# Strassen's seven block products for the first product of the second expert layer, in three of its five token blocks

## The chip, the cores and the metric

One Trainium2 chip, one core of it. The metric is device time of one execution in microseconds (us), lower is better. The engines are named as the profile names them: PE is TensorE's matmul, PEld its weight load, DVE VectorE, ACT ScalarE, POOL GpSimd, SP the engine whose queue issues most transfers.

## What is computed

```
a = attention(q, k, v, M_prev, z_prev, beta)     # 4 x 8 heads, 576 tokens, 64 wide
x = a as 2304 tokens x 512
h = x @ w_in;   x = (h * cos(h)) @ w_out         # first expert layer: 512 -> 2048 -> 512
h = x @ w2_in;  r = max(h, 0)
out = (r * r) @ w2_out                           # second expert layer, the same shapes
```

All of it is in float32. A float32 product is made of three fp32r matmuls: each operand is split into a part that fp32r holds exactly (hi) and the rest (lo), and hi·hi, hi·lo and lo·hi are summed in PSUM.

## The kernel before

Attention runs first and takes until about 193 us; the two layers follow. The 2304 tokens lie in five blocks of 512, 512, 512, 256 and 512 (`CFG['sizes']`), the 2048 hidden features in 16 f-tiles of 128. A **step** (`steps`, line 280) is a layer, a block and an f-tile. Phase 1, the first layer, is steps 0 to 79; phase 2, the second layer, is steps 80 to 159, its blocks in the order 0, 1, 2, 4, 3 (`order2`, line 69), so the block of 256 tokens comes last.

In a step `l1` (line 293) makes the first product: for each of four slices of 128 input features three matmuls of 128 x n into `h`, n being the block's tokens; twelve in all. Then comes a chain on ACT and DVE (`g_a` to `g_g`, lines 318 to 369). In phase 2 this is `relu` on ACT, its square on DVE, the hi part `gh` on ACT, and `gl = gf - gh` on DVE. Two steps later (`skew`) `l2` (line 863) adds the f-tile's part of the second product into four PSUM banks `a0` to `a3`, which hold 128 tokens x 512 each in phase 2: twelve matmuls of 512 columns, or six for the block of 256 tokens. After a block's last f-tile `evac` (line 901) copies these to SBUF and stores them.

The order of the instructions on each engine is written out: for every step the templates in `CFG['tpl']` list tokens (L1, a, b, f, g, L2 and so on, each with a lag in steps), and `_Pinned` (line 34) keeps each engine in the order of the calls. So nearly every instruction has line 48. Weights of the second layer are converted from float64 words during phase 1, stored to DRAM and loaded again, split (`split_hi`, `split_lo`) in steps 64 to about 83, and then stay in SBUF: `winh`, `winl`, `wouth`, `woutl` for each f-tile. The activations between the layers go through DRAM (`x1T`); `x_load`, `x_hi` and `x_lo` (lines 240 to 273) bring a block's 512 features back as four `xh`/`xl` pairs.

Of the kernel before, what the change touches and what calls it, by code (L numbers as in the profile page):

```python
# [33 lines left out]
class _Pinned:  # L34
# [5 lines left out]
    def __getattr__(self, name):  # L40
# [83 lines left out]
def kernel(  # L124
# [15 lines left out]
    S = (qk.shape[3] - 128) // 2  # L140
    NT, DM = out.shape
# [117 lines left out]

    def x_hi(phase, j, kk, raw):  # L260
        n = blocks[j][1]
        hi = xs.tile([128, 512], F32R, tag=f"xh{kk}", name=f"xh{kk}")
        lo = xs.tile([128, 512], F32R, tag=f"xl{kk}", name=f"xl{kk}")
        act.activation(out=hi[:, span(n)], in_=raw[:, 0:n], func=AF.Copy)
        xt[phase, j, kk] = (hi, lo)
        return hi, lo, raw, n
# [4 lines left out]
            out=lo[:, span(n)], in0=raw[:, 0:n], in1=hi[:, span(n)].bitcast(F32), op=ALU.subtract  # L271
        )

    ps_s = ctx.enter_context(tc.tile_pool(name="ps_s", bufs=2, space=PSUM))
# [6 lines left out]
    opens = {(p, j, a) for p, j, a, e in segs}  # L281
    closes = {(p, j, e - 1) for p, j, a, e in segs}
    xneed, s0 = {}, 0
    for p, j, a, e in segs:
        if a == 0 and s0:
# [573 lines left out]
    def moe(ctx, g_o, early):  # L859
        ps_a = ctx.enter_context(tc.tile_pool(name="psa", bufs=1, space=PSUM))  # L860
        acc, part = {}, {}

        def l2(s):
            p, j, f = steps[s]
            n = blocks[j][1]
            hi, lo = wt[p, "out", f]
            gh, gl = gs.pop(s)
            na = KD if p == 1 else n // 128
            if (p, j, f) in opens:
                for c in range(na):  # L870
                    acc[c] = ps_a.tile([128, 512], F32, tag=f"a{c}", name=f"a{c}")
            for c in range(na):
# [13 lines left out]

        def evac_tile(c):
            if c < 2:
                return g_o.tile([128, 512], F32, tag="ob", name="ob")
            return wr.tile([128, 512], F32, tag="wl", name="ob", bufs=2)  # L890

        got = {}
# [8 lines left out]
        def evac(s):  # L901
# [4 lines left out]
            for c in range(KD if p == 1 else n // 128):  # L906
                cs = slice(c * 128, (c + 1) * 128)
                w = n if p == 1 else DM
                if s == len(steps) - 1 and c == n // 128 - 1:
                    for x, e in enumerate((sync, act)):  # L910
                        hc = slice(x * 256, (x + 1) * 256)
                        ob = evac_tile(2 + x)
                        copy("D", ob[:, hc], acc[c][:, hc])
                        e.dma_start(out=out[t0 + c * 128:t0 + (c + 1) * 128, hc], in_=ob[:, hc])
                    continue
                if (j, c) in got:
                    ob = got.pop((j, c))
                    dve.tensor_tensor(out=ob, in0=acc[c], in1=ob, op=ALU.add)
                else:
                    ob = evac_tile(c)  # L920
# [9 lines left out]
        for e in (pe, act, dve, pool, sync):  # L930
            e.last = None
        SK = CFG["skew"]
        N = len(steps)
# [5 lines left out]
        raws, convs, stores, backs, xs_at = [], {}, {}, {}, {}  # L939
# [24 lines left out]
        def step(name, u, s):  # L964
            live = u < N
            if name == "L1":
                if live and u >= early:
                    l1(u)
            elif name == "L2":
                if live:  # L970
                    l2(u)
                    l2_done.add(u)
            elif name in "abcdsefg":
                if live:
                    g_do(name, u)
            elif name == "k0":
                if raws and u in plan:
                    it, raw = raws.pop(0)
                    convs[u] = (it, *c_steps(raw), {})
            elif name[0] == "k":  # L980
                if u in convs:
                    it, wf, ops, made = convs[u]
                    x = int(name[1])
                    assert all(y in made for y in {2: (1,), 3: (2,), 4: (3,), 6: (4, 5)}.get(x, ()))
                    made[x] = True
                    ops[x - 1]()
                    if name == "k6" and s + 1 < free_at(it):
                        stores[u] = convs.pop(u)
            elif name in ("h0", "h1", "h2", "o0", "o1", "o2"):
                src = convs if name[1] == "0" else backs  # L990
                key = u if name[1] == "0" else (u, int(name[1]))
                if key in src:
                    it, wf, made = src[key][0], src[key][1], src[key][-1]
                    if name[0] == "h":
                        assert name[1] != "0" or 6 in made
                        made["h"] = split_hi(it[0], wf, it[1], it[2])
                    else:
                        split_lo(it[0], wf, made["h"], it[1], it[2], CFG["lo"][it[0] - 1])
            elif name == "ld":
                raw_next()  # L1000
            elif name in ("r1", "r2"):
# [102 lines left out]
```

## Time and profile before

| | before |
|---|---|
| time, median of 3 runs (lowest, highest) | 981.21 us (980.02, 981.24) |
| time of the profiled execution | 980.61 us |
| span of that execution (first to last instruction) | 978.9 us |
| PE busy | 971.3 us (99%), 5454 matmuls |
| DVE, ACT, POOL busy | 588.5 us (60%), 542.3 us (55%), 166.0 us (17%) |
| moved by DMA | 95.87 MB, mean 98 GB/s |

How to read it: "busy" of PE counts a matmul until its modelled end, so matmuls that follow each other overlap in it; the time that a matmul costs is the distance from its start to the next one's. In a row of the timeline the first number is the start, the second the duration. A bracket at the end gives the idle time before it and what ended it.

### The profile page before, as it was taken

The page shows a single profiled execution, that of the slowest core. Times are in us where ns is not written, and L with a number is a line of the kernel's source. Part 1 is how long each engine was busy: PE and PEld are TensorE (multiplying, and loading weights), DVE is VectorE, ACT ScalarE, POOL GpSimd, SP SyncE. Part 2 cuts the span into 40 slices and gives each one's busy share as a digit, 9 for nine tenths or more (in the row PEclk, how much of TensorE's full clock was granted, in tenths as well). Part 3 has the DMA queues.
Part 4 walks back from the last instruction along what each step waited for, and adds up shares of the span by engine and source line. Part 5 has one row for each costly group of instructions (what it writes and reads, how often), then busy time and mean ns, then how long its engine had stood idle before and what let it go on. Part 6 is the DMA issues. An engine that isn't in the chain of part 4 may idle for free.

```text
span 978.9 us, 14925 instructions
## 1 busy us (share of the span) xinstructions
PE 971.3 (99%) x5454; PEld 796.6 (81%) x5454; DVE 588.5 (60%) x1249; ACT 542.3 (55%) x1135; POOL 166.0 (17%) x247
## 2 busy tenths in 40 slices
PE   8999999999999999999999999999999999999998
PEld 5777777788888888889988888888888888888897
DVE  7988888588899667678887885323232323222232
ACT  7999998777777656666767773222222222222222
POOL 7777875300111000001000000000000000000000
PEclk9999999999999999999999999999999999999999
DMA  6345654453324433343355552001000100100010
GB/s 196 125 166 187 214 194 144 159 151 108 107 86 138 143 108 108 104 144 126 123 172 153 181 167 82 22 0 65 10 13 1 65 21 2 54 1 12 1 44 22
DMA packets 54699, 95.87 MB, mean 98 GB/s; under 512 B 5730, under 2 KB 26722, under 8 KB 54626
## 3 DMA queue, kind: packets, MB, share of 16 engines
q1 hardware_dynamic: 54192, 94.50, 29.8%
q8 instruction: 43, 0.70, 0.3%
q10 hardware_dynamic: 434, 0.43, 0.1%
q14 instruction: 30, 0.25, 0.1%
HBM read 70.00 MB, written 24.90 MB: 97 GB/s over the span
## 4 chain that ended last, share of the span: by engine, by line
PE 95%; DVE 3%; ACT 1%; issue 1%; DMA 0%; DVEq 0%; POOL 0%; POOLq 0%
PE h L48 39%; PE a L48 39%; PE o L48 6%; PE sps L48 5%; PE ptps L48 5%; PE qps L48 2%; DVE gf L48 1%; DVE wa L48 1%; DVE P L48 0%; DVE wb L48 0%; ACT gf L48 0%; DMA x1T<-ob 0%; ACT ki L48 0%; ACT P L48 0%; ACT gh L48 0%
## 5 line engine op out<-in xcount | busy, mean ns | idle before, releaser
L48 PE MATMUL h<-xh,winh 128*128 128x512 f32 (+1 forms) x640 | 236.0, 369 | 0.2 <-DVE gf L48 0.2
L48 PE MATMUL h<-xh,winl 128*128 128x512 f32 (+1 forms) x640 | 235.0, 367 | 0.0
L48 PE MATMUL h<-xl,winh 128*128 128x512 f32 (+1 forms) x640 | 235.0, 367 | 0.0
L48 DVE TENSOR_TENSOR gf<-gf 128x512 f32<-128x512 f32 (+1 forms) x80 | 51.1, 639 | 269.9 <-ACT gf L48 269.9
L48 ACT ACTIVATE gf<-h 128x512 f32<-128x512 f32 (+1 forms) x80 | 44.4, 556 | 287.2 <-PE h L48 287.2
L48 PEld LDWEIGHTS h<-xh,winh 128*128 128x128 f32 x640 | 120.2, 188 | 21.5 <-DVE gf L48 0.6
L48 PEld LDWEIGHTS h<-xl,winh 128*128 128x128 f32 x640 | 120.1, 188 | 20.4
L48 PEld LDWEIGHTS h<-xh,winl 128*128 128x128 f32 x640 | 120.5, 188 | 19.9
L48 PE MATMUL a<-gl,wouth 128*128 128x512 f32 (+1 forms) x320 | 117.8, 368 | 0.1
L48 PE MATMUL a<-gh,wouth 128*128 128x512 f32 (+1 forms) x319 | 117.1, 367 | 0.3 <-DVE ob L48 0.3
L48 PE MATMUL a<-gh,woutl 128*128 128x512 f32 (+1 forms) x320 | 117.4, 367 | 0.0
L48 PE MATMUL a<-woutl,gh 128*128 128x512 f32 x288 | 112.0, 389 | 0.0
L48 PE MATMUL a<-wouth,gl 128*128 128x512 f32 x288 | 112.0, 389 | 0.0
L48 PE MATMUL a<-wouth,gh 128*128 128x512 f32 x288 | 112.0, 389 | 0.0
L48 ACT ACTIVATE gh<-gf 128x512 fp32r<-128x512 f32 (+1 forms) x160 | 93.4, 584 | 33.1 <-DVE gf L48 32.1
L48 DVE TENSOR_TENSOR gl<-gf,gh 128x512 fp32r<-128x512 f32 (+1 forms) x158 | 102.0, 645 | 4.2 <-ACT gh L48 2.5
L48 POOL TENSOR_SCALAR wa<-wa 128x512 f32<-128x512 f32 x63 | 40.0, 634 | 364.8 <-ACT wa L48 334.8
L48 POOL TENSOR_SCALAR P<-P,sm 128x384 f32<-128x384 f32 (+3 forms) x128 | 87.0, 697 | 29.2 <-ACT x L48 20.1
L48 ACT ACTIVATE ki<-h 128x512 int32<-128x512 f32 (+1 forms) x80 | 44.2, 552 | 64.7 <-PE h L48 64.3
L48 DVE TENSOR_TENSOR gf<-h,gf 128x512 f32<-128x512 f32 (+1 forms) x80 | 50.7, 634 | 47.6 <-ACT ki L48 41.0
L48 ACT ACTIVATE P<-P,mx 128x384 f32<-128x384 f32 (+3 forms) x128 | 70.5, 560 | 2.5 <-DVE mx L45 2.5
L48 PEld LDWEIGHTS a<-gl,wouth 128*128 128x128 f32 x320 | 60.1, 188 | 10.8 <-DVE gl L48 0.6
(95 smaller groups left out, 1478.9 us busy)
## 6 DMA issues: line engine op xcount, KB each, us to landing
wraw<-in_moe_w_in_dram SPq DMA_DIRECT2D x32, 512.0 KB, 4.1
wraw<-in_moe_w_out_dram SPq DMA_DIRECT2D x32, 512.0 KB, 3.8
qk<-in_qk_dram SPq DMA_DIRECT2D x15, 640.0 KB, 5.3
vr<-in_vrow_dram SPq DMA_DIRECT2D x16, 320.0 KB, 5.6
xT<-x SPq DMA_DIRECT2D x16, 288.0 KB, 2.3
out_dram<-ob SPq DMA_DIRECT2D x17, 256.0 KB, 2.2
x1T<-ob SPq DMA_DIRECT2D x16, 256.0 KB, 2.3
xraw<-x1T SPq DMA_DIRECT2D x16, 256.0 KB, 3.1
```

The lines of the kernel that those rows point to most:

```text
L48: made = call(*args, **kwargs)
```

## The change

In phase 2 the blocks come in the order 0, 3, then 1, 2, 4. Blocks 0 and 3 are steps 80 to 111 (`NS` is 112) and run as before. For blocks 1, 2 and 4 (512 tokens each) the first product is made for two f-tiles at a time: the 256 hidden features x 512 input features by 512 input features x 512 tokens are cut into 2 x 2 blocks of 256, and seven products of these blocks (Winograd's variant) give the result in place of eight. There are 8 pairs per block, 24 in all, numbered k.

Beside that: the sums of weight blocks (s1 to s4) are made on POOL during steps 85 to 100 from the stored weights, split by ACT and DVE into hi and lo, and stored to DRAM (`s_load` to `s_store`). For this every second-layer w_in tile is now stored. In the pairs of the first block s1 is loaded over the weight half that is no longer needed (`s_place`), and for every pair 768 KB of s2, s3 and s4 come back through two sets of buffers (`r_load`). The sums of activation blocks (t1 to t4) are made on POOL (`t_make`), for the first block in steps 105 to 108, for the other two during the block before, and split on ACT and DVE (`x_h`, `x_l`). All x tiles live in one SBUF tile `xb`. The four PSUM banks that held `h` become `h0` to `h3` of 256 columns each; `combine` adds up products that PSUM can't add itself, and `g_sq` does relu and square in one DVE instruction.

```diff
-       'order2': [0, 1, 2, 4, 3],
+       'order2': [0, 3],
+       'seven': [1, 2, 4],
...
+    xb = xs.tile([128, 14 * 512 + 64], F32R, name="xb", bufs=1)
...
+        def s_sum(q):
+            wa, wb = sums[q]
+            t = [g_p.tile([128, 512], F32, tag="ki", name="sf") for _ in range(2)]
+            a11, a12, a21, a22 = wa[:, 0:256], wa[:, 256:512], wb[:, 0:256], wb[:, 256:512]
...
+            for o, x, y, op in (
+                (s1, a21, a22, ALU.add), (s2, s1, a11, ALU.subtract),
+                (s3, a11, a21, ALU.subtract), (s4, a12, s2, ALU.subtract),
+            ):
+                pool.tensor_tensor(out=o, in0=x, in1=y, op=op)
...
+        def s_split(q):
...
+            for x, h, _ in hl:
+                act.activation(out=h, in_=x, func=AF.Copy)
+            for x, h, l in hl:
+                dve.tensor_tensor(out=l, in0=x, in1=h.bitcast(F32), op=ALU.subtract)
...
+        def s_place(q):
+            hi, lo = wt[2, "in", 2 * q]
+            sync.dma_start(out=hi[:, 0:256].bitcast(F32), in_=spilled["s", q, 2][:, 0:256])
+            sync.dma_start(out=lo[:, 0:256].bitcast(F32), in_=spilled["s", q, 2][:, 256:512])
...
+        def r_load(k):
+            q = k % (NF // 2)
+            r1 = wr.tile([128, 2 * DM], F32R, tag="wraw", name="r1")
+            r2 = wr.tile([128, DM], F32R, tag="wa", name="r2", bufs=2)
+            sync.dma_start(out=r1.bitcast(F32), in_=spilled["s", q, 0])
+            sync.dma_start(out=r2.bitcast(F32), in_=spilled["s", q, 1])
...
+        def product(k, i):
+            w, x, bank, first = {
+                1: ("a11", "b11", k % 2, True), 2: ("a12", "b21", 2, True), 7: ("s3", "t3", 3, True),
+                6: ("s2", "t2", k % 2, False), 4: ("a22", "t4", 3, False), 5: ("s1", "t1", k % 2, False),
+                3: ("s4", "b22", k % 2, False),
+            }[i]
...
+            for kt in range(2):
+                ws, xc = slice(128 * kt, 128 * kt + 128), slice(256 * kt, 256 * kt + 256)
+                for n, (lt, rt) in enumerate(((wh, xh), (wh, xl), (wl, xh))):
+                    pe.matmul(
+                        out=banks[bank], lhsT=lt[:, ws], rhs=rt[:, xc],
...
+        def combine(k, x):
+            a, c, d = banks[k % 2], banks[2], banks[3]
+            if x == "c11":
+                ha[k] = g_p.tile([128, 512], F32, tag="gf", name="ha")
+                act.activation(out=ha[k][:, 0:256], in_=c, func=AF.Copy)
+                dve.tensor_tensor(out=ha[k][:, 0:256], in0=a, in1=ha[k][:, 0:256], op=ALU.add)
+            elif x == "p7":
+                p7[k] = wr.tile([128, DM], F32, tag="wc", name="p7", bufs=1)
+                act.activation(out=p7[k][:, 0:256], in_=d, func=AF.Copy)
+            elif x == "u2":
+                act.activation(out=p7[k][:, 256:512], in_=a, func=AF.Copy)
+            elif x == "c21":
+                hb[k] = g_p.tile([128, 512], F32, tag="ki", name="hb")
+                dve.tensor_tensor(out=hb[k][:, 0:256], in0=d, in1=p7[k][:, 256:512], op=ALU.add)
+            elif x == "c22":
+                dve.tensor_tensor(out=hb[k][:, 256:512], in0=a, in1=p7[k][:, 0:256], op=ALU.add)
+            else:
+                act.activation(out=ha[k][:, 256:512], in_=a, func=AF.Copy)
...
+            dve.scalar_tensor_tensor(out=h, in0=h, scalar=0.0, in1=h, op0=ALU.max, op1=ALU.mult)
...
+        for k in range(K):
+            s0 = NS + 2 * k
...
+            if k + 1 < KP:
+                s_place(k + 1)
+            if 0 < k and k + 1 < K:
+                r_load(k + 1)
...
+            if k > 0:
+                combine(k - 1, "c12")
+            product(k, 1)
+            if k > 0:
+                g_sq(k - 1, 1)
+            product(k, 2)
+            combine(k, "c11")
...
+            product(k, 7)
+            combine(k, "p7")
...
+            l2(s0 - 2)
...
+            product(k, 6)
+            combine(k, "u2")
+            product(k, 4)
+            combine(k, "c21")
...
+            l2(s0 - 1, (0, .5))
+            evac(s0 - 1, (0, .5))
+            product(k, 5)
+            combine(k, "c22")
...
+            g_sq(k, 0)
...
+            if k < K - 1:
+                l2(s0 - 1, (.5, 1))
+                evac(s0 - 1, (.5, 1))
+            product(k, 3)
+            if k == K - 1:
+                l2(s0 - 1, (.5, 1))
...
+            g_do("f", s0)
+            g_do("g", s0)
```

Three places show how the instructions move. The first is PE's order for a first product in block 1. Before, one f-tile's product has twelve such rows; these are the first six (two of the four slices of input features).

```order
L48 MATMUL h<-xh_5992,winh_5966 128x512
L48 MATMUL h<-xl_5993,winh_5966 128x512
L48 MATMUL h<-xh_5992,winl_5988 128x512
L48 MATMUL h<-xh_6109,winh_5966 128x512
L48 MATMUL h<-xl_6110,winh_5966 128x512
L48 MATMUL h<-xh_6109,winl_5988 128x512
```

Now, products 2 and 7 of a pair (bank `h2`, then bank `h3`; `r1` and `r2` are the loaded sums of weights):

```order
L48 MATMUL h2_7660<-xb_79,winh7_6052 128x256 x2
L48 MATMUL h2_7660<-xb_79,winl7_6070 128x256
L48 MATMUL h2_7660<-xb_79,winh7_6052 128x256 x2
L48 MATMUL h2_7660<-xb_79,winl7_6070 128x256
L48 MATMUL h3_7661<-xb_79,r1_7846 128x256 x2
L48 MATMUL h3_7661<-xb_79,r2_7847 128x256
L48 MATMUL h3_7661<-xb_79,r1_7846 128x256 x2
L48 MATMUL h3_7661<-xb_79,r2_7847 128x256
```

A product is six matmuls of 256 columns, so a pair has 42 of these in place of 24 of 512 columns, with the second product's matmuls of 512 columns between them.

The second place is the hand-over inside a pair, on PE and DVE. On PE: product 5 into bank `h0`, half of a second product, and product 3 into the same bank, which waits for DVE.

```order
L48 MATMUL h0_7658<-xb_79,winh4_5880 128x256 [waits DMAHW3_49,Activation_49]
L48 MATMUL h0_7658<-xb_79,winh4_5880 128x256
L48 MATMUL h0_7658<-xb_79,winl4_5898 128x256 [waits DMAHW4_49]
L48 MATMUL h0_7658<-xb_79,winh4_5880 128x256 x2
L48 MATMUL h0_7658<-xb_79,winl4_5898 128x256
L48 MATMUL a2_7791<-wouth3_5935,gh_7867 128x512
L48 MATMUL a2_7791<-wouth3_5935,gl_7869 128x512
L48 MATMUL a2_7791<-woutl3_5957,gh_7867 128x512
L48 MATMUL a3_7795<-wouth3_5935,gh_7867 128x512
L48 MATMUL a3_7795<-wouth3_5935,gl_7869 128x512
L48 MATMUL a3_7795<-woutl3_5957,gh_7867 128x512
L48 MATMUL h0_7658<-xb_79,r1_7742 128x256 [waits DVE_49]
```

On DVE in a pair: the sum c21, the sum c22 (which reads the bank between products 5 and 3), the square, `gl`, and the same for the other f-tile.

```order
L48 TENSOR_TENSOR hb_7909<-h3_7661,p7_7877 128x256 [waits PE_49,Activation_49]
L48 TENSOR_TENSOR hb_7909<-h0_7658,p7_7877 128x256 [waits PE_49]
L48 SCALAR_TENSOR_TENSOR hb_7909<-hb_7909 128x512 [waits DVE_49]
L48 TENSOR_TENSOR gl_7939<-hb_7909,gh_7937 128x512 [waits Activation_49]
L48 SCALAR_TENSOR_TENSOR ha_7864<-ha_7864 128x512 [waits Activation_49]
L48 TENSOR_TENSOR ha_7961<-h1_7659,ha_7961 128x256 [waits Activation_49]
L48 TENSOR_TENSOR gl_7966<-ha_7864,gh_7964 128x512 [waits Activation_49]
```

Before, DVE had two squares and two `gl` here. Three reads of PSUM are new, and PE waits for one of them between two products of the same bank.

The third place is SP's queue. Before, in block 1 of phase 2, it held the next block's four x tiles and the last one's outputs:

```order
L48 DMA xraw_6701<-x1T1_75 128x512
L48 DMA xraw_6769<-x1T1_75 128x512
L48 DMA xraw_6837<-x1T1_75 128x512
L48 DMA xraw_6905<-x1T1_75 128x512
L48 DMA out_0_dram<-ob_7097 128x512
L48 DMA out_0_dram<-ob_7100 128x512
```

Now, for two pairs of the first seven-product block:

```order
L48 DMA winh6_5996<-sw3_2_7028 128x256 [waits DMAHW3_49]
L48 DMA winl6_6018<-sw3_2_7028 128x256 [waits DMAHW4_49]
L48 DMA r1_7846<-sw3_0_7024 128x1024 [waits DMAHW5_49,PE_49]
L48 DMA r2_7847<-sw3_1_7026 128x512 [waits DMAHW6_49,PE_49]
L48 DMA winh8_6106<-sw4_2_7115 128x256 [waits DMAHW7_49]
L48 DMA winl8_6124<-sw4_2_7115 128x256 [waits DMAHW0_49]
L48 DMA r1_7943<-sw4_0_7111 128x1024 [waits DMAHW1_49,PE_49]
L48 DMA r2_7944<-sw4_1_7113 128x512 [waits DMAHW2_49,PE_49]
```

A stage in which the queue was almost empty now loads 768 KB for every pair, and in the first of the three blocks 256 KB more; each load of `r1` waits until PE is done with the buffer's last user.

## Rows read from the trace of the kernel before

**Rows 1.** The page: span, busy time by engine, and the chain that ended last.
```profile
span 978.9 us, 14925 instructions
...
PE 971.3 (99%) x5454; PEld 796.6 (81%) x5454; DVE 588.5 (60%) x1249; ACT 542.3 (55%) x1135; POOL 166.0 (17%) x247
...
PE 95%; DVE 3%; ACT 1%; issue 1%; DMA 0%; DVEq 0%; POOL 0%; POOLq 0%
```

**Rows 2.** Windows, busy us and instructions by engine, granted clock, DMA share, GB/s.
```profile
540.00:604.00 64.00, 64.00 (x284) 53.01 (x283) 51.17 (x85) 43.58 (x78) 3.08 (x5) 1.00 0.49 158
604.00:925.00 321.00, 321.00 (x1417) 265.77 (x1417) 89.06 (x141) 76.70 (x140) 0.00 (x0) 1.00 0.06 20
925.00:972.00 47.00, 47.00 (x301) 42.82 (x300) 13.58 (x34) 12.45 (x34) 0.00 (x0) 1.00 0.06 23
```

**Rows 3.** Timeline of PE, phase 2: where groups of twelve 512-column matmuls start.
```profile
908.91 0.39 PE L48 MATMUL h<-xh,winh 128*128 128x512 f32 x1
...
911.63 0.39 PE L48 MATMUL a<-wouth,gh 128*128 128x512 f32 x1
...
914.35 0.39 PE L48 MATMUL h<-xh,winh 128*128 128x512 f32 x1
```

**Rows 4.** Timeline, phase 2, block of 256 tokens: twelve matmuls, six, and the chain behind.
```profile
950.14 0.28 PE L48 MATMUL h<-xh,winh 128*128 128x256 f32 x1
...
951.43 0.28 PE L48 MATMUL h<-xh,winl 128*128 128x256 f32 x1
951.55 0.39 PE L48 MATMUL a<-wouth,gh 128*128 128x512 f32 x1
...
951.75 0.38 ACT L48 ACTIVATE gf<-h 128x256 f32<-128x256 f32 x1 [2.08 <-PE h L48]
...
952.16 0.43 DVE L48 TENSOR_TENSOR gf<-gf 128x256 f32<-128x256 f32 x1 [2.01 <-ACT gf L48]
...
952.91 0.28 PE L48 MATMUL h<-xh,winh 128*128 128x256 f32 x1
```

**Rows 5.** Timeline, phase 1, block of 256 tokens: a late wait, then undisturbed groups of twelve.
```profile
464.67 0.19 PEld L48 LDWEIGHTS a<-gl,wouth 128*128 128x128 f32 x1 [0.28 <-DVE gl L48]
...
466.12 0.39 PE L48 MATMUL h<-xh,winh 128*128 128x256 f32 x1
466.34 0.28 PE L48 MATMUL h<-xl,winh 128*128 128x256 f32 x1
466.46 0.28 PE L48 MATMUL h<-xh,winl 128*128 128x256 f32 x1
...
468.97 0.28 PE L48 MATMUL h<-xh,winh 128*128 128x256 f32 x1
...
470.33 0.28 PE L48 MATMUL a<-gh,wouth 128*128 128x256 f32 x1
```

**Rows 6.** Groups by form: count, busy us and mean ns of one, idle time before.
```profile
L48 DVE TENSOR_TENSOR gl<-gf,gh 128x512 fp32r<-128x512 f32 x126 | 86.7, 688 | 3.2 <-ACT gh L48 1.5
L48 ACT ACTIVATE gh<-gf 128x512 fp32r<-128x512 f32 x128 | 80.2, 627 | 26.4 <-DVE gf L48 26.1
...
L48 ACT ACTIVATE gh<-gf 128x256 fp32r<-128x256 f32 x32 | 13.2, 414 | 6.6 <-DVE gf L48 6.0 <-PE a L48 0.7
...
L48 DVE TENSOR_TENSOR gf<-h,gf 128x256 f32<-128x256 f32 x16 | 6.7, 422 | 4.5 <-ACT ki L48 2.8 <-ACT gf L48 1.4
...
L48 ACT ACTIVATE gf<-h 128x256 f32<-128x256 f32 x16 | 6.1, 384 | 34.8 <-PE h L48 34.8
...
L48 POOL TENSOR_TENSOR woutl<-wa,wouth 128x512 fp32r<-128x512 f32 x4 | 6.0, 1506 | 0.0
```

**Rows 7.** DMA issues: tile, queue, count, KB each, median us to landing.
```profile
wraw<-in_moe_w_in_dram SPq DMA_DIRECT2D x32, 512.0 KB, 4.1
...
wf<-ws2in SPq DMA_DIRECT2D x15, 256.0 KB, 2.6
```

More of the change, by code (lines that the diff above doesn't have):

```diff
@@ L261, in x_hi @@
         n = blocks[j][1]
-        hi = xs.tile([128, 512], F32R, tag=f"xh{kk}", name=f"xh{kk}")
-        lo = xs.tile([128, 512], F32R, tag=f"xl{kk}", name=f"xl{kk}")
+        if (phase, n) == (2, 256):
+            base = 512 * 10 + 256 * kk
+            hi, lo = xb[:, base:base + 304], xb[:, base + 1024:base + 1328]
+        else:
+            base = 512 * (kk + 8 * (phase == 1 and j in (1, 2, 4)))
+            hi = xb[:, base:base + 512]
+            if base + 2048 < 14 * 512:
+                lo = xb[:, base + 2048:base + 2560]
+            else:
+                lo = xs.tile([128, 512], F32R, tag="xe", name="xe")
         act.activation(out=hi[:, span(n)], in_=raw[:, 0:n], func=AF.Copy)
@@ L272, in x_lo @@
         )
-    ps_s = ctx.enter_context(tc.tile_pool(name="ps_s", bufs=2, space=PSUM))
+    hctx = ctx.enter_context(ExitStack())
+    ps_s = hctx.enter_context(tc.tile_pool(name="ps_s", bufs=2, space=PSUM, side="right"))
     hs = {}
@@ L280 @@
     steps = [(p, j, f) for p, j, a, e in segs for f in range(a, e)]
-    opens = {(p, j, a) for p, j, a, e in segs}
-    closes = {(p, j, e - 1) for p, j, a, e in segs}
+    NS = len(steps)
+    segs7 = [(2, j, 0, NF) for j in CFG["seven"]]
+    steps += [(p, j, f) for p, j, a, e in segs7 for f in range(a, e)]
+    opens = {(p, j, a) for p, j, a, e in segs + segs7}
+    closes = {(p, j, e - 1) for p, j, a, e in segs + segs7}
     xneed, s0 = {}, 0
@@ L905, in evac @@
             t0, n = blocks[j]
-            for c in range(KD if p == 1 else n // 128):
+            na = KD if p == 1 else n // 128
+            for c in range(int(span_[0] * na), int(span_[1] * na)):
                 cs = slice(c * 128, (c + 1) * 128)
@@ L932, in moe @@
         SK = CFG["skew"]
-        N = len(steps)
+        N = NS
         L0 = (NB - 1) * NF
@@ L988, in step @@
                         stores[u] = convs.pop(u)
+                    elif name == "k6" and it[:2] == (2, "in"):
+                        copies[u] = convs[u]
             elif name in ("h0", "h1", "h2", "o0", "o1", "o2"):
@@ L1017, in step @@
                     store(it[0], it[1], it[2], wf)
+                elif u in copies:
+                    it, wf = copies[u][0], copies[u][1]
+                    store(it[0], it[1], it[2], wf)
             elif name == "xd":
@@ new lines, in s_store @@
+        def s_store(q):
+            for x, r in enumerate(sums.pop(q)):
+                d = dram.tile([128, 2 * DM if x == 0 else DM], F32, name=f"sw{q}_{x}")
+                sync.dma_start(out=d, in_=r.bitcast(F32))
+                spilled["s", q, x] = d
+        def s_place(q):
+            hi, lo = wt[2, "in", 2 * q]
+            sync.dma_start(out=hi[:, 0:256].bitcast(F32), in_=spilled["s", q, 2][:, 0:256])
+            sync.dma_start(out=lo[:, 0:256].bitcast(F32), in_=spilled["s", q, 2][:, 256:512])
@@ new lines, in b_load @@
+        def b_load(j, x):
+            i, h = int(x[1]) - 1, int(x[2]) - 1
+            if x in ("b11", "b21"):
+                t = xs.tile([128, S], F32, tag="xraw", name="xraw")[:, 0:512]
+            else:
+                t = wr.tile([128, DM], F32, tag="wb", name="xraw")
+            sync.dma_start(
+                out=t.rearrange("p (k c) -> p k c", k=2),
+                in_=x1T[j][256 * i:256 * (i + 1), 256 * h:256 * (h + 1)].rearrange("(k p) c -> p k c", p=128),
+            )
+            stage[j, x] = t
@@ new lines, in x_l, with weights @@
+        def x_l(j, x):
+            dve.tensor_tensor(out=xpart(x, 1), in0=stage[j, x], in1=xpart(x, 0).bitcast(F32), op=ALU.subtract)
+        ha, hb, p7 = {}, {}, {}
+        def weights(k, x):
+            q = k % (NF // 2)
+            hb_, lb_ = wt[2, "in", 2 * q]
+            ha_, la_ = wt[2, "in", 2 * q + 1]
+            r1, r2 = ring[k]
+            return {
+                "a11": (ha_[:, 0:256], la_[:, 0:256]), "a12": (ha_[:, 256:512], la_[:, 256:512]),
+                "a22": (hb_[:, 256:512], lb_[:, 256:512]), "s1": (hb_[:, 0:256], lb_[:, 0:256]),
+                "s2": (r1[:, 0:256], r1[:, 768:1024]), "s3": (r1[:, 256:512], r2[:, 0:256]),
+                "s4": (r1[:, 512:768], r2[:, 256:512]),
+            }[x]
@@ new lines, in product @@
+        def product(k, i):
[4 more added lines that the diff above has]
+            }[i]
+            wh, wl = weights(k, w)
+            xh, xl = xpart(x, 0), xpart(x, 1)
+            for kt in range(2):
[3 more added lines that the diff above has]
+                        out=banks[bank], lhsT=lt[:, ws], rhs=rt[:, xc],
+                        start=(first and kt == 0 and n == 0), stop=(kt == 1 and n == 2),
+                        skip_group_check=True,
+                    )
@@ new lines, in g_sq, with at @@
+        def g_sq(k, odd):
+            h = (ha if odd else hb)[k]
+            rs[NS + 2 * k + odd] = h
+            dve.scalar_tensor_tensor(out=h, in0=h, scalar=0.0, in1=h, op0=ALU.max, op1=ALU.mult)
+        order7 = [j for j in CFG["seven"]]
+        KP = NF // 2
+        extra = {}
+        def at(s, fn, *a):
+            extra.setdefault(s, []).append((fn, a))
+        for q in range(KP):
+            when = ((84 + 2 * q, 1, 2, 3), (94, 1, 3, 4), (96, 1, 4, 5), (98, 2, 4, 5))[max(0, q - 4)]
+            for d, fn in zip((0, *when[1:]), (s_load, s_sum, s_split, s_store)):
+                at(when[0] + d, fn, q)
@@ new lines, in moe @@
+        at(108, s_place, 0)
+        j7 = order7[0]
+        for s, xs_ in ((102, ("b11", "b12")), (103, ("b21", "b22"))):
+            for x in xs_:
+                at(s, b_load, j7, x)
+        for s, x in ((105, "t1"), (106, "t2"), (107, "t3"), (108, "t4")):
+            at(s, t_make, j7, x)
+        at(107, r_load, 0)
+        at(109, r_load, 1)
+        for s, x in ((106, "b11"), (107, "b21"), (108, "t2"), (109, "t3"), (110, "t4"), (111, "t1")):
+            at(s, x_h, j7, x)
+            at(s, x_l, j7, x)
@@ L1042 @@
+        combine(K - 1, "c12")
+        g_sq(K - 1, 1)
+        g_do("f", NS + 2 * K - 1)
+        g_do("g", NS + 2 * K - 1)
+        l2(NS + 2 * K - 2)
+        l2(NS + 2 * K - 1)
+        evac(NS + 2 * K - 1)
     with ExitStack() as actx:
```

96 lines of the change are left out of this document (85 added, 11 removed).

## The prediction

> **What bounds the kernel.** I read the page first [rows 1]: PE is busy for 99% of the span and carries 95% of the chain that ended last. So only what PE issues, or what makes it wait, can move the time. Next the windows [rows 2]: from 604 to 925 us, the four 512-token blocks of phase 2, PE is busy for 321.00 of 321.00 us at the full granted clock (1.00, the 2.4 GHz level), while ACT and DVE are busy for about a quarter, POOL not at all, and DMA moves 20 GB/s. The work that the change adds goes to the four that have room. The work that it takes away is PE's. Last the timeline of PE, for what one matmul costs: a busy share can't show it, the distance between starts can.
>
> **Matmuls removed and added.** In a 512-token block a first product starts at 908.91 us, the second product behind it at 911.63, and the next first product at 914.35 [rows 3]. So twelve matmuls of 512 columns take 2.72 us, 226.7 ns each, and two f-tiles' first products take 24 x 226.7 ns = 5.44 us. A pair now takes 42 matmuls of 256 columns. By columns alone that is 21/24, or 7/8.
>
> What a 256-column matmul costs has two answers in this trace. In phase 2's block of 256 tokens, where such a group of twelve stands between 512-column matmuls, it takes 951.55 - 950.14 = 1.41 us, 117.5 ns each [rows 4]; its other groups are alike. In phase 1, where 256-column groups follow each other, undisturbed ones take 470.33 - 468.97 = 1.36 us, 113.3 ns each [rows 5]. The pairs mix 256- and 512-column matmuls as rows 4 do, so I take 117.5 ns: 42 x 117.5 = 4.94 us, 0.50 us less per pair, 24 x 0.50 = **12.0 us** less in all. The other end, 113.3 ns, gives 4.76 us and 24 x 0.68 = 16.3 us.
>
> The Trainium skill ("TensorE: Matmul & The Clock Gate", section "Back-to-back issue gap") gives N/2.4 + 2.5 ns between isolated warm matmuls, 215.8 and 109.2 ns here; worked out from that page, as an estimate, the saving would be 24 x (24 x 215.8 - 42 x 109.2) ns = 14.2 us. The trace differs with 226.7 and 117.5 ns, and the measurement decides.
>
> The second products (24 x 12 x 2 matmuls of 512 columns) stay. The 256-token block moves, with the same matmuls and two-step lag; nothing of its PE time changes.
>
> **The new hand-overs in a pair.** PE now waits for ACT or DVE before products 6, 4, 5 and 3, because PSUM banks are read between products. The reads cost 384 ns on ACT and 422 ns on DVE, by the nearest reads of 256 columns [rows 6]. From the last matmul's start to ACT's start is 951.75 - 951.43 = 0.32 us, and from ACT's start to DVE's 0.41 us [rows 4]. So c22 is done about 0.32 + 0.42 + 0.03 = 0.77 us after product 5's last start. Half a second product (6 x 226.7 ns = 1.36 us) plus that last matmul's 0.12 us cover it: 1.48 us, so it costs nothing, with 0.7 us to spare. Without this cover it would cost 0.65 us per pair. In pair 0 the half is three matmuls and the cover is 0.80 us, just enough. For u2 between products 6 and 5 the cover is product 4 and a half, 2.07 us; for c11 and p7 it is a whole second product and more.
>
> The longer chain is c22, square, `gh`, `gl`, then the second product. Its end is about 0.32 + 0.42 + 0.69 + 0.63 + 0.69 us [rows 6], with three hand-overs of 0.03 us some 2.85 us after product 5. PE meanwhile has 1.36 us of second product and four products (24 x 117.5 ns = 2.82 us), 4.2 us together. What else is queued there: ACT has four reads and two `gh` per pair, 4 x 0.38 + 2 x 0.63 = 2.8 us, and DVE three sums, two squares and two `gl`, 3 x 0.42 + 4 x 0.69 = 4.0 us, of a pair's 4.94 + 5.44 = 10.4 us. In the two pairs that also split the next block's x tiles, six times 0.63 us on ACT and 0.69 us on DVE come on top: 6.6 and 8.1 us, still under 10.4.
>
> **The one uncovered place** is the last pair. There product 3 follows product 5 directly, since the half is kept to cover the chain behind it. PE waits 0.77 - 0.12 = 0.65 us there, and the first weight load after a wait isn't hidden, +0.1 us by the 0.22 us between the first two starts at 466.12 [rows 5]: **+0.8 us** (bounds 0.4 and 1.6, the latter if the chain behind is late as well). The output's tail is the same as before.
>
> **Side work in steps 84 to 111.** The weight sums cost POOL four additions per pair of f-tiles, at most 1.5 us each (1506 ns for a twice as long one, rows 6), 6 us, every 5.4 us or more and mostly alone. Nothing needs them before the pairs start, and POOL had nothing to do. The splits add 0.63 + 2 x 0.41 = 1.45 us to ACT and about 1.55 us to DVE in eight steps. In the block of 256 tokens a step lasts 952.91 - 950.14 = 2.77 us [rows 4], and ACT's own work is 0.38 + 0.41 us, DVE's 0.43 + 0.42: 2.3 and 2.4 us together, so they fit. The fullest is step 97, which also copies out block 0 (two copies each): about 3.5 us on ACT and 3.8 on DVE, of a step that lasts 2.72 + 1.41 = 4.13 us, as its second product still has 512 tokens. I cost it at 0 (up to 1.5).
>
> **Loads.** A pair loads 768 KB on SP's queue, in the first block 256 KB more. `r_load` starts when product 3 two pairs earlier is done and is needed one pair and two products later, 10.4 + 1.4 = 11.8 us. A 512 KB load took 4.1 us and a 256 KB one 2.6 us [rows 7], one after the other 9.3 us for 1 MB; with several under way, 158 GB/s flowed from 540 to 604 us with PE still fully busy [rows 2], which makes 6.6 us. Behind them on the queue stand only the next block's x loads and outputs, which are not urgent. Cost 0.
>
> **Sum.** The profiled execution took 980.61 us: 980.61 - 12.0 + 0.8 = 969.4 us. The runs' median is 981.21, 0.6 higher, so for a median **970.0 us**. A measurement of this kernel can tell about 0.2%, or 2 us, from no change.
>
> **Rivals.**
> 1. *The faster spacing.* If the long runs of 256-column matmuls (products 3, 1, 2, 7 make 24 in a row) go at 113.3 ns, 16.3 us are saved: 965.7 us. Against it: each run follows 512-column matmuls, as in rows 4. Chance 0.11.
> 2. *Hand-overs or side work a little late.* If the chains run behind by 0.1 to 0.3 us per pair, 2.4 to 7.2 us are lost: 972.4 to 977.2 us. For it: ACT and DVE keep strict order, and waits on late reads did stop PE in phase 1 [rows 5]. Against it: margins of 0.7 us or more. Chance 0.16.
> 3. *Weight loads exposed: slower.* Behind a late wait the next weight load isn't hidden, and starts lie 0.22 us apart in place of 0.11 [rows 5]. A pair has up to ten matmuls with a wait of their own (before products 7, 6, 4, 5, 3 and the second products, and for lo parts). Should each product's start cost this 0.11 us though its wait is over, six make 0.66 us per pair, 0.16 more than is gained: 24 x 0.16 = 3.8 us, 985.8 us in place of 970.0; with all ten it would be 996. It decides from 0.50 / 0.11 = 4.5 such starts per pair. Against it: groups in rows 3 and 4 start behind waits too, and their distances are even. Chance 0.09. By the Trainium skill (the same page, section "LDWEIGHTS (loading the stationary operand)") loading 128 columns takes 128/1.2 = 107 ns, as long as a 256-column matmul streams and half as long as a 512-column one, which speaks against halving the matmuls; rows 4 with 117.5 ns show it still nearly hidden.
> 4. *The ring of loads late: slower.* It decides where 1 MB takes over 11.8 us (below 89 GB/s); at 70 GB/s seven pairs of 15 us in place of 10.4 would lose 32 us: 1002 us. Chance 0.04.
>
> **Chances.** Forecast 0.60 (969 to 971.5), rivals 0.11, 0.16, 0.09, 0.04. Faster by over 0.2%: 0.60 + 0.11 + 0.16 = 0.87. Of the 0.13 for rivals 3 and 4 some 0.03 falls within 0.2%, when about four starts per pair are exposed, and 0.10 is slower. The range takes in the forecast, rival 1 and most of rival 2: 965.0 to 975.5 us.
>
> **What the new profile would show.** Right: PE's matmuls rise by 24 x 18 = 432; a pair repeats every 10.4 us; groups of six 256-column matmuls take 0.70 us; the only PE idle time of phase 2 is 0.7 us near the end. Wrong: PE waits with DVE `hb` or ACT `p7` as releaser in every pair (rival 2), starts 0.22 us apart at the products' beginnings (rival 3), waits for DMA `r1` or `r2` (rival 4), or a pair of 10.2 us (rival 1).

## The result and the profile after

The changed kernel takes **970.8 us** (median of 4 runs, 970.07 to 971.94); the kernel before took 980.71 us beside it (4 runs, 980.02 to 981.24). The ratio is 0.990, with a 95% interval of 0.9883 to 0.9918: faster by about 10 us. The profiled execution took 970.63 us, its span 968.9 us, against 980.61 and 978.9 us before.

The page's lines that answer to [rows 1], and the loads of the weight sums:

```profile
span 968.9 us, 16203 instructions
...
PE 960.5 (99%) x5886; PEld 807.7 (83%) x5886; DVE 650.4 (67%) x1354; ACT 564.6 (58%) x1216; POOL 209.0 (22%) x291
...
PE 95%; DVE 3%; ACT 1%; issue 1%; DMA 0%; DVEq 0%; POOL 0%; POOLq 0%
...
r<-sw SPq DMA_DIRECT2D x24, 512.0 KB, 3.8
...
r<-sw SPq DMA_DIRECT2D x24, 256.0 KB, 4.0
```

PE has 432 matmuls more and 10.8 us less busy time, and still carries 95% of the chain. The windows answer to [rows 2]: the steps with the side work, then the pairs.

```profile
648.00:714.00 66.00, 66.00 (x392) 58.67 (x392) 34.95 (x64) 24.56 (x61) 18.25 (x20) 1.00 0.49 168
...
720.00:955.00 235.00, 235.00 (x1496) 213.87 (x1495) 105.27 (x177) 68.33 (x156) 12.27 (x8) 1.00 0.31 100
```

PE is busy for all of both stretches, at the same granted clock of 1.00 (the 2.4 GHz level), while DVE's share has grown from 28 to 45% in the pairs and DMA moves 100 GB/s in place of 20. That is a busy share, though. Whether a matmul got dearer is read from the chain of waits (start, duration, engine, product, number of matmuls). One whole pair of it:

```profile
937.06 2.83 PE h L48 x24
939.89 2.72 PE a L48 x12
942.61 1.41 PE h L48 x12
944.02 1.36 PE a L48 x6
945.38 0.71 PE h L48 x6
946.09 1.36 PE a L48 x6
947.45 2.83 PE h L48 x24
```

The pair repeats every 10.39 us. Its 42 matmuls of 256 columns take 2.83 + 1.41 + 0.71 = 4.95 us, 117.8 ns each, and the second products 226.7 ns each, exactly as in [rows 3, 4]. All 24 pairs read like this, but for the first and the last. The saving is 24 x (5.44 - 4.944) = 11.9 us.

**Where the rest went.** 11.9 us were saved and 10.0 show in the span. Four losses and one shift make up the difference. First, who PE's weight loads waited for from 600 us on (us in total, times, longest):

```profile
PEld h L48 <- DVE hb L48: 1.0, 2, 0.7
PEld a L48 <- DVE gl L48: 0.3, 1, 0.3
```

Two waits for `hb` and one for `gl`, in 369 us. In the chain of waits they stand here: step 97's second product, pair 0, and the last pair with the hand-over from product 5 to product 3.

```profile
674.22 1.36 PE a L48 x6
...
677.00 1.62 PE a L48 x6
...
718.84 2.94 PE h L48 x24
...
955.77 0.72 PE h L48 x6
956.49 0.02 issue
956.51 0.44 DVE hb L48
956.95 0.04 issue
956.99 0.97 PE h L48 x6
```

- The last pair: from product 5's start to the second product behind product 3 it is 957.96 - 955.77 = 2.19 us in place of 1.41: +0.78.
- Pair 0: 2.94 in place of 2.83 us: +0.11. The half of three matmuls does not quite cover the hand-over.
- Step 97: 1.62 in place of 1.36 us: +0.25. DVE was late with `gl`.
- The tail, from the last matmul's start to the span's end: 968.9 - 964.39 = 4.51 us; before it was 978.9 - 974.84 = 4.06: +0.45. Most of it comes with POOL's weight sums and not with the outputs, as the experiment on the tail shows.
- The shift: step 90's first product starts at 631.90 us in this execution and at 631.63 in the one of before. PE's program is the same up to there, and this start varied between 631.04 and 633.13 us over the fourteen profiles of this study. So these +0.27 us can't be put down to the change.

The sum: -11.9 + 0.78 + 0.11 + 0.25 + 0.45 + 0.27 = -10.04 us, where the spans differ by 10.0.

Step 97 is worth a look in the timeline, since nothing in it should have been late:

```profile
673.46 1.90 DVE L48 TENSOR_TENSOR r<-sf,r 128x512 fp32r<-128x512 f32 x3
674.22 0.85 POOL L48 TENSOR_TENSOR sf<-wf 128x256 f32<-128x256 f32 x1 [12.07 <-DVE r L48]
...
675.15 0.80 POOL L48 TENSOR_TENSOR sf<-sf,wf 128x256 f32<-128x256 f32 x1
675.28 0.95 DVE L48 TENSOR_TENSOR gf<-gf 128x256 f32<-128x256 f32 x1
675.92 0.91 POOL L48 TENSOR_TENSOR sf<-wf 128x256 f32<-128x256 f32 x1
676.16 0.95 DVE L48 TENSOR_TENSOR gl<-gf,gh 128x256 fp32r<-128x256 f32 x1
...
677.17 0.19 PEld L48 LDWEIGHTS a<-wouth,gl 128*128 128x128 f32 x1 [0.26 <-DVE gl L48]
...
677.62 0.43 DVE L48 TENSOR_TENSOR gf<-gf 128x256 f32<-128x256 f32 x1 [0.51 <-ACT gf L48]
```

The same square of 256 columns takes 0.95 us beside POOL's additions and 0.43 us in the next step without them. The late `gl` is not too much work on DVE but slower work.

### The profile page after: what moved, and what is told of

The parts are those of the page before. It is cut to its first block, busy times and chain, and to the rows that moved or that the text cites. A ratio compares the mean times of both kernels' runs of the same rounds, so it can differ in the third digit from the quotient of the medians.

```text
span 968.9 us, 16203 instructions
## 1 busy us (share of the span) xinstructions
PE 960.5 (99%) x5886; PEld 807.7 (83%) x5886; DVE 650.4 (67%) x1354; ACT 564.6 (58%) x1216; POOL 209.0 (22%) x291
## 4 chain that ended last, share of the span: by engine, by line
PE 95%; DVE 3%; ACT 1%; issue 1%; DMA 0%; DVEq 0%; POOL 0%; POOLq 0%
PE a L48 39%; PE h L48 38%; PE o L48 6%; PE sps L48 5%; PE ptps L48 5%; PE qps L48 2%; DVE gf L48 1%; DVE wa L48 1%; DVE P L48 0%; DVE wb L48 0%; ACT gf L48 0%; DMA x1T<-ob 0%; ACT ki L48 0%; ACT P L48 0%; ACT gh L48 0%
## 5 line engine op out<-in xcount | busy, mean ns | idle before, releaser
L48 PE MATMUL h<-xb,winh 128*128 128x256 f32 (+1 forms) x1184 | 293.6, 331 | 0.2 <-DVE gf L48 0.2
L48 PEld LDWEIGHTS h<-xb,winh 128*128 128x128 f32 x1184 | 202.2, 188 | 24.9 <-DVE gf L48 0.4
L48 PE MATMUL h<-xb,winl 128*128 128x256 f32 (+1 forms) x640 | 214.3, 335 | 0.0
L48 PEld LDWEIGHTS h<-xb,winl 128*128 128x128 f32 x640 | 121.2, 189 | 12.6
L48 DVE TENSOR_TENSOR hb<-h,p 128x256 f32<-128x256 f32 x48 | 20.4, 425 | 98.8 <-PE h L48 98.8
L48 ACT ACTIVATE gh<-gf 128x512 fp32r<-128x512 f32 (+1 forms) x112 | 63.4, 566 | 32.5 <-DVE gf L48 32.0
L48 DVE TENSOR_TENSOR gl<-gf,gh 128x512 fp32r<-128x512 f32 (+1 forms) x110 | 71.6, 651 | 3.4 <-ACT gh L48 1.6
L48 PEld LDWEIGHTS a<-gh,wouth 128*128 128x128 f32 x319 | 59.9, 188 | 10.6 <-DVE ob L48 0.7
L48 PEld LDWEIGHTS a<-gh,woutl 128*128 128x128 f32 x320 | 60.2, 188 | 10.1
L48 PE MATMUL sps<-qk 64*128 64x384 f32 (+4 forms) x320 | 63.1, 456 | 1.6 <-DVE mx L48 1.1
```

Source lines behind the costliest of these rows:

```text
L48: made = call(*args, **kwargs)
```

## The experiments

My theory was that of the prediction: a pair's saving is set by the spacing of the 256-column matmuls, the half second product covers the bank's hand-over, and the rest lies beside PE. The rivals were exposed weight loads, another limit just behind, and costs of the move or of the side work. The kernel before took 980.66, 981.05 and 980.87 us in the three series.

**The move alone** (`e1_move`), on the kernel before:

```diff
-       'order2': [0, 1, 2, 4, 3],
+       'order2': [0, 3, 1, 2, 4],
```

> The kernel before with only the block order of phase 2 changed to 0, 3, 1, 2, 4. Theory (the saving is all in the pairs; the move costs only its tail): PE's time in phase 2 is unchanged, and the end comes about 0.4 us later after the last matmul, because the last block now has four outputs of 256 KB close together in place of two (4.5 against 4.1 us from the last matmul's start to the end): 980.7 + 0.4 = 981.1 us, which can't be told from no change. Rival (the move itself pays, the products give less than the groups' starts show): 978 us or lower.

Measured: 982.61 us, ratio 1.0019 (1.001 to 1.0029), 1.95 us slower: far more than expected. The last matmul starts at 974.89 us, 974.84 before, so PE lost nothing; the time is behind it, in the tail:

```profile
975.32 0.42 DVE L48 COPY ob<-a 128x256 f32<-128x256 f32 x1 [0.67 <-PE a L48]
977.54 0.42 DVE L48 COPY ob<-a 128x256 f32<-128x256 f32 x1 [1.80 <-DMA out_dram<-ob]
```

The two halves of the last output take two buffers of a ring of two. With a block of four outputs the ring is already in use, and the second half waits 1.80 us for a store. The change puts both halves into one buffer. Whether that is the whole cause, `e9_move1` tested:

```diff
+                    ob = evac_tile(c)
                     for x, e in enumerate((sync, act)):
                         hc = slice(x * 256, (x + 1) * 256)
-                        ob = evac_tile(2 + x)
```

> The kernel before with its blocks in the order 0, 3, 1, 2, 4, as e1_move, but with both halves of the last output in one buffer, as the change has it. Theory: the block's move costs nothing on PE, and e1_move lost its 1.95 us only because the second half's copy waited 1.80 us for a store to free a buffer; now that copy follows the first at once, the tail from the last matmul's start is 4.1 to 4.6 us in place of 5.7, and the time is 0 to 0.5 us over the kernel before (980.7 to 981.5). Rival: the move itself loses time in steps 80 to 112; then it stays at about 982.6.

Measured: 981.12 us, ratio 1.0003 (0.9994 to 1.0012). Both halves are copied at once, and the tail is 979.1 - 974.93 = 4.17 us:

```profile
975.36 0.75 DVE L48 COPY ob<-a 128x256 f32<-128x256 f32 x2 [0.67 <-PE a L48]
976.14 0.38 ACTq L48 DMA_DIRECT2D out_dram<-ob  x1
```

The move is free, given that one line of the diff.

**The cover taken away** (`e2_nocover`): product 3 directly behind product 5 in every pair, the half second product after it.

```diff
-            if k < K - 1:
-                l2(s0 - 1, (.5, 1))
-                evac(s0 - 1, (.5, 1))
             product(k, 3)
-            if k == K - 1:
-                l2(s0 - 1, (.5, 1))
+            l2(s0 - 1, (.5, 1))
+            evac(s0 - 1, (.5, 1))
```

> The changed kernel with product 3 directly behind product 5 in every pair, the half of a second product moved behind it. Theory (the half is the cover of DVE's read between the two products): PE stands still 0.65 us and exposes one weight load (0.1 us) in each of the other 23 pairs, as it does in the last pair now (2.19 us for what lasts 1.41): 970.8 + 23 x 0.78 = 988.7 us, and PE's wait for DVE hb is named 24 times. Rival (the work behind a waiting matmul is pulled ahead, or the read is hidden anyway): under 973 us.

Measured: 988.65 us, ratio 1.0081 (1.0066 to 1.0096), as expected, and slower than the kernel before. The wait of the last pair now stands in all 24:

```profile
PEld h L48 <- DVE hb L48: 17.3, 24, 0.7
```

So the place of one half second product decides between 10 us won and 8 us lost.

**What lies behind** (`e3_drop4`): product 4 is left out, so that the output lacks its part.

```diff
-            product(k, 4)
```

> The changed kernel without product 4: six products per pair, so one block of the result is incomplete. Theory (only PE's issue bounds the pairs, at 117.8 ns per 256-column matmul): 24 x 6 x 117.8 ns = 17.0 us less, 953.8 us, a pair of 9.68 us, and no new wait of PE. Rival (ACT, DVE, or the loads of 768 KB to 1 MB per pair are a bound just behind PE): less than 14 us gained, with PE waiting for r1, r2, hb or p7 in every pair.

Measured: 953.5 us, ratio 0.9723 (0.9706 to 0.9739). With 0.71 us less per pair the time falls by 17.3 us, 24 x 0.71 = 17.0, and only a single new wait of 0.2 us appears. So no load and no chain on ACT or DVE lies within those 0.71 us per pair behind PE.

**The start column** (`e4_off0`, `e10_off16`, `e10_off64`). The 256-column parts of the x tiles begin at column 48 of their place in `xb`, as the operands of the block of 256 tokens did in the kernel before. I moved the start to 0, and then to 16 and 64:

```diff
-            return xb[:, 48 + 512 * (2 * slot[x] + lo):48 + 512 * (2 * slot[x] + lo + 1)]
+            return xb[:, 512 * (2 * slot[x] + lo):512 * (2 * slot[x] + lo + 1)]
```

> The changed kernel with the x parts of the seven products starting at column 0 of xb in place of column 48. Theory (256-column matmuls beside 512-column ones cost 117.8 ns whatever their start): 970.8 us, groups of six 0.71 us. Rival (the start address sets whether they cost 117.8 or 113.3 ns, or more): 966 us, or some us above 971 if the address 48 is what keeps them at 117.8.

Measured: 974.22 us, ratio 0.9934 (0.9919 to 0.9949). My theory was wrong here: 3.4 us of the gain hang on the start column. A pair lasts 950.91 - 940.37 = 10.54 us; the 24 matmuls take 2.87 us in place of 2.83, and the twelve 512-column matmuls behind them 2.75 in place of 2.72:

```profile
940.37 2.87 PE h L48 x24
943.24 2.75 PE a L48 x12
...
950.91 2.87 PE h L48 x24
```

> The changed kernel with the 256-column parts of the x tile from column 16 in place of 48. e4_off0 took 10.54 us for a pair from column 0 in place of 10.38. Theory A: only a start on a full 256 columns costs; then 16 is as good as 48: a pair of 10.38 us, 970.8 us. Theory B: the start's distance from it counts; then a pair takes between 10.38 and 10.54 us, and the time lies at 972 to 974.

Measured: 972.59 us, ratio 0.9914 (0.9901 to 0.9928), a pair of 10.48 us: theory B.

```profile
938.44 2.83 PE h L48 x24
941.27 2.75 PE a L48 x12
...
948.92 2.83 PE h L48 x24
```

> The changed kernel with the 256-column parts of the x tile from column 64 in place of 48. Theories A and B of e10_off16 both give a pair of 10.38 us and 970.8 us. Rival C: it is the remainder by 64 columns that counts (48 has one, 0 and 64 have none); then a pair takes 10.54 us again, 974.2 us.

Measured: 975.53 us, ratio 0.9944 (0.993 to 0.9957), a pair of 10.54 us again: rival C, not A and not B. (In this profile PE also waited 1.1 us once for DVE `xb`, outside the pairs compared.) So a start at 0 and at 64 costs 0.15 us per pair, at 16 it costs 0.10, at 48 the least of the four. Rival C is not the whole answer either, as 16 has a remainder by 64 too. From column 0, more than half of the 0.15 us lies in the 512-column matmuls: the three groups of 256-column ones take 2.87 + 1.43 + 0.71 = 5.01 us in place of 4.95, the three of 512-column ones 2.75 + 1.39 + 1.39 = 5.53 in place of 5.44. Of the twelve in a row only the first six are slower, 944.47 - 943.08 = 1.39 us from the first to the seventh start in `e4_off0` and 1.36 for the other six. Why is open; only these four columns were tried, all on 256-column operands.

**The last pair** (`e5_last`): in the last pair the half that stood before product 6 and the one kept for later change places, so that one lies between products 5 and 3.

```diff
+            if k == K - 1:
+                l2(s0 - 2, (0, .5))
+                product(k, 6)
+                combine(k, "u2")
+                product(k, 4)
+                combine(k, "c21")
+                l2(s0 - 2, (.5, 1))
+                product(k, 5)
+                combine(k, "c22")
+                g_sq(k, 0)
+                l2(s0 - 1, (0, .5))
+                product(k, 3)
+                l2(s0 - 1, (.5, 1))
```

> The last pair's instructions in another order: half of a second product stands between products 5 and 3, and the half that was kept for later behind product 3. Theory: the 0.78 us that PE waits there (DVE hb) is all that is wrong in that place, and the chain behind product 5 (about 2.85 us) is covered by two halves and product 3 (3.4 us): 0.8 us less than the changed kernel, 970.0 us; the weight load's idle time with DVE hb as releaser falls from 1.0 to about 0.3 us (pair 0 alone). Rival: the chain behind is late instead, a wait for DVE gl of 0.4 to 0.8 us takes its place, and the time stays at 970.8.

Measured: 970.22 us, ratio 0.9891 (0.9873 to 0.9908). The `hb` wait of 0.7 us is gone and no `gl` wait came for it:

```profile
PEld h L48 <- DVE hb L48: 0.3, 1, 0.3
PEld a L48 <- DVE gl L48: 0.3, 1, 0.3
```

**The tail** (`e6_lasttail`): besides, the last two second products go by output column.

```diff
-        l2(NS + 2 * K - 2)
-        l2(NS + 2 * K - 1)
-        evac(NS + 2 * K - 1)
+        l2(e, (0, .75))
+        l2(o, (0, .75))
+        evac(o, (0, .75))
+        l2(e, (.75, 1))
+        l2(o, (.75, 1))
+        evac(o, (.75, 1))
```

> As e5_last, and the last two second products go by output column: three of four columns of both, whose outputs are then copied and stored, and the fourth column of both last. Theory: the tail of 4.51 us from the last matmul's start to the span's end (4.06 in the kernel before) is longer because four outputs of 256 KB are stored within 2 us; with three of them 1.4 us earlier the tail is about 4.1: 0.3 to 0.45 us less than e5_last, 969.6 us. Rival: the tail is set by the last copy and its own store alone; then it stays at 4.5 and the time at e5_last's.

Measured: 969.45 us, ratio 0.9882 (0.9867 to 0.9898). The tail is 967.6 - 963.37 = 4.23 us, `e5_last`'s 967.3 - 962.73 = 4.57: 0.34 less, as expected. By the slices of the DMA view its packets end 2.6 us behind the last matmul's start in place of 2.9. But the reason given for the longer tail, four outputs close together, is mostly wrong. In `e8_dvesum` (below), which stores the same four outputs in the changed kernel's order, the tail is 968.5 - 964.41 = 4.09, and in `e9_move1`, also with four outputs, 4.17. The last matmuls of the changed kernel and of `e8_dvesum`:

```profile
964.39 0.39 PE L48 MATMUL a<-woutl,gh 128*128 128x512 f32 x1
```

```profile
964.41 0.39 PE L48 MATMUL a<-woutl,gh 128*128 128x512 f32 x1
```

The packets end 2.9 us behind these starts in both, 2.8 in the kernel before. What differs is the time from there to the span's end. It is 1.6 to 1.7 us in all nine profiles of kernels whose weight sums are on POOL, and 1.2 to 1.3 us in the five others (the kernel before, `e1_move`, `e9_move1`, `e8_dvesum`, `e11_best`). So of the tail's +0.45 us about 0.1 are the stores', by that coarse view, and most comes with the weight sums on POOL. Why they lengthen an end that lies over 250 us behind them is not shown.

**POOL beside DVE** (`e7_q6`, `e8_dvesum`). First I tried to put the weight sums of pair 6 one step later:

```diff
-            when = ((84 + 2 * q, 1, 2, 3), (94, 1, 3, 4), (96, 1, 4, 5), (98, 2, 4, 5))[max(0, q - 4)]
+            when = ((84 + 2 * q, 1, 2, 3), (94, 1, 3, 4), (96, 2, 4, 5), (98, 2, 4, 5))[max(0, q - 4)]
```

> The changed kernel, with the weight sums of pair 6 on POOL one step later (step 98 in place of 97), so that in step 97 POOL adds nothing beside DVE's work on the block of 256 tokens. Theory: the 256-column additions and subtractions on DVE, 0.95 us beside POOL's, fall to 0.42 us there, PE's wait for DVE gl of 0.3 us at 677 us goes, and the time is 0.3 us less: 970.5 us. In step 98 POOL has two pairs' sums, 7.3 us, which nobody waits for. Rival: step 97 is late because of its two more copies out of PSUM; then DVE's rows stay or PE still waits 0.2 to 0.3 us, and the time is 970.8.

Measured: 970.56 us, ratio 0.9894 (0.9878 to 0.9909), inconclusive: the edit moved nothing. POOL had nothing else to do and began the additions at 674.15 us as before, when DVE's splits had freed their buffer. The step in which an instruction is written down does not hold back an engine that is idle. The profile has a second wait for `gl`, which the changed kernel's lacks: it is for pair 1's `gl`, while POOL makes activation sums:

```profile
730.41 1.29 POOL L48 TENSOR_TENSOR xt<-xraw,xt 128x512 f32<-128x512 f32 x1 [1.06 <-DMA xraw<-x1T]
...
730.59 1.66 DVE L48 TENSOR_TENSOR gl<-hb,gh 128x512 fp32r<-128x512 f32 x1 [0.70 <-ACT gh L48]
...
732.30 0.19 PEld L48 LDWEIGHTS a<-wouth,gl 128*128 128x128 f32 x1 [0.38 <-DVE gl L48]
```

The subtraction took 1.66 us in place of 0.69: the same slowing. Here the time at which an x tile lands decides whether it happens. Then the same sums on DVE, so that POOL is idle:

```diff
-                pool.tensor_tensor(out=o, in0=x, in1=y, op=op)
+                dve.tensor_tensor(out=o, in0=x, in1=y, op=op)
```

> The changed kernel, with the weight sums on DVE in place of POOL. Theory: DVE's 256-column subtractions take 0.95 us because POOL works at the same time; with POOL idle they take 0.42 to 0.43 us in every step of the block of 256 tokens, and a sum takes 0.42 us on DVE in place of 0.91 on POOL. DVE's own work in a step rises by 1.7 us and falls by about 1.0: within 0.5 us of 970.8. Rival: the 0.95 us come from the x tile layout or the operands in these steps; then they stay at 0.95, DVE's work in a step rises to over 4.1 us, and PE waits for gl in several steps: 971.5 to 973.

Measured: 970.12 us, ratio 0.9889 (0.9873 to 0.9905). The groups by form from 640 to 700 us, first of the changed kernel, then of this one (busy us, mean ns):

```profile
L48 DVE TENSOR_TENSOR gl<-gf,gh 128x256 fp32r<-128x256 f32 x10 | 6.4, 636 | 0.0
L48 DVE TENSOR_TENSOR r<-sf,r 128x256 fp32r<-128x256 f32 x10 | 6.0, 637 | 0.0
```

```profile
L48 DVE TENSOR_TENSOR gl<-gf,gh 128x256 fp32r<-128x256 f32 x10 | 4.2, 417 | 0.0
...
L48 DVE TENSOR_TENSOR r<-sf,r 128x256 fp32r<-128x256 f32 x10 | 3.8, 420 | 0.0
```

With POOL idle the operations take 0.42 us again, so the operands are not to blame. The wait for `gl` at step 97 is gone: from block 0's first copy on DVE to the last pair's first product it is 947.47 - 671.75 = 275.72 us, against 947.45 - 671.49 = 275.96 in the changed kernel, 0.24 us less. The three splits take 1.35 us in place of 1.90:

```profile
673.72 1.35 DVE L48 TENSOR_TENSOR r<-sf,r 128x512 fp32r<-128x512 f32 x3
```

With the 0.42 us that the tail is shorter, 0.66 us are gained, where the medians differ by 0.68. The expectation had only "within 0.5 us", as it did not have the tail. Twenty more additions on DVE in these steps (of the 32 in all) cost PE nothing.

**All three together** (`e11_best`): `e6_lasttail`'s and `e8_dvesum`'s edits in one kernel.

> e6_lasttail and e8_dvesum together: last pair in the other order, the last outputs spread, the weight sums on DVE. Theory: the three savings lie in different places and add up: against the changed kernel 0.7 us in the last pair, 0.3 us at step 97 and 0.3 us in the tail, 969.4 - 0.3 = 969.1 us; PE's weight load waits once more for DVE (hb, pair 0, 0.3 us) and not for gl. Rival: the weight sums make DVE late elsewhere, and it stays at 969.4 or above.

Measured: **968.98 us**, ratio 0.9877 (0.9864 to 0.9891): 1.8 us under the changed kernel and the fastest of those that compute everything. PE's weight loads wait for DVE once (`hb`, pair 0, 0.3 us). The tail is 967.9 - 964.12 = 3.78 us: `e6_lasttail`'s 0.3 and `e8_dvesum`'s 0.4 us are both in it. The parts add up: 0.78 for the last pair, 0.24 for step 97 and 4.51 - 3.78 = 0.73 for the tail make 1.75 us, and 1.8 came.

## Why the prediction was right, and where its terms were off

- *The matmuls:* 12.0 us forecast at 117.5 ns, 11.9 us came at 117.8. `e3_drop4` shows that this price holds when a product more is taken away. The other end, 113.3 ns (rival 1), did not come: the pairs have the distances of rows 4, not those of rows 5. What the prediction did not know is that the 117.5 ns of rows 4 hold for a start at column 48: from column 0 the saving would have been 3.4 us smaller. That the new operands start there too was no part of its reasoning: to that extent the price came out by luck.
- *The hand-overs:* 1.36 us of cover for 0.65 us, cost 0. That held in 23 pairs, and `e2_nocover` confirmed the price without the cover: (988.65 - 970.8) / 23 = 0.78 us, where the prediction said 0.65 plus 0.1 for the exposed weight load. For pair 0 "just enough" was slightly too kind: +0.11 us.
- *The one uncovered place:* +0.8 forecast, +0.78 measured, and `e5_last` took it away.
- *Side work, "I cost it at 0 (up to 1.5)":* the term was mis-sized, by 0.25 us. The step that failed is the sum of 3.8 us for DVE in step 97, of durations taken from steps in which POOL is idle. Beside POOL's additions the three splits took 1.90 us in place of 1.35, the square and `gl` 0.95 each in place of 0.42: about 1.6 us more. With the two copies at 0.69 us, DVE's step is 2 x 0.69 + 1.90 + 2 x 0.95 = 5.2 us in a step of 4.13. Rival 2's "margins of 0.7 us or more" did not hold for this step by the prediction's own sum, which left 0.33 us, nor for pair 0, which had 0.03: these two are the places where PE waited beyond the forecast.
- *"The output's tail is the same as before":* 4.51 us against 4.06. Wrong as a step: the term was put at nothing and measured 0.45 us. About 0.1 of it are the stores of the last block, which has four outputs where two stood before; most of it comes with the weight sums on POOL (`e8_dvesum`: 4.09), so it belongs to the side work as well. `e1_move` shows that it could have been 2 us, had the diff not put both halves into one buffer, a line that I passed over.
- *The move and the loads:* 0 and 0. `e9_move1` shows the first, and 235.00 of 235.00 us with loads of 3.8 and 4.0 us the second (rival 4 did not come). No start of a product is exposed (rival 3): the 24 matmuls of four products in a row last 24 x 117.8 ns.

The forecast of 969.4 us for the profiled execution and its 970.63 us differ by 1.2: 0.25 + 0.11 + 0.45 + 0.27 + 0.1, all of the same sign, and 0.27 of them lie in front of the steps that changed on PE.

## What to carry to other kernels

On an engine that is busy all the time, the distance between starts times the count is the forecast; read it from the stage whose neighbours look most like the new ones, and check that the operands lie alike, down to the start column. A product that reuses a PSUM bank needs other matmuls between: half a second product was worth 18 us here. Before work is given to an idle POOL, look at what DVE does beside it, and add up DVE's step at the slower price.

## What the runs showed of the hardware

**POOL's additions slow DVE's.** An operation of DVE with both inputs in SBUF took 0.95 us beside POOL's additions and 0.42 without (256 columns), 1.66 and 0.69 (512 columns). One that reads PSUM and one SBUF operand kept its time while POOL was adding; in the changed kernel, pair 2:

```profile
732.17 1.75 POOL L48 TENSOR_TENSOR xraw<-xraw 128x512 f32<-128x512 f32 x1
732.69 0.41 DVE L48 TENSOR_TENSOR ha<-h,ha 128x256 f32<-128x256 f32 x1
```

The ends fit two engines that take turns: at step 97 POOL's third addition ends at 675.92 + 0.91 = 676.83 us and DVE's `gl`, begun before that, 0.28 us later, less than the 0.42 us that it takes alone. The Trainium skill ("SBUF — State Buffer", section "Who interferes with whom") says that a DVE instruction with two SBUF inputs contends with a GpSimd instruction that reads SBUF, and that the port pair they share is an exclusive lock. These rows agree with it.

**The start column of the moving operand counts.** Four starts of the same 256-column operands gave pairs of 10.54 (0), 10.48 (16), 10.39 (48) and 10.54 us (64), 1.5% between the ends, and the 512-column matmuls behind them, whose own operands had not moved, became slower by 1% too (2.75 against 2.72 us for twelve).

**POOL's weight sums lengthen the program's end.** From the last store's packets to the end of the span it took 1.6 to 1.7 us in the nine profiles with these sums on POOL and 1.2 to 1.3 us in the five without, though the sums ended over 250 us earlier. The two pairs that differ in this alone, the changed kernel and `e8_dvesum`, `e6_lasttail` and `e11_best`, have tails of 4.51 and 4.09, 4.23 and 3.78 us.
